# Softmax factors transposed by VectorE in 32 by 32 blocks instead of by TensorE

## The chip, the cores and the metric

The kernel runs on one core of a Trainium2 chip. A core has five engines, each with its own stream of instructions, which run side by side and wait for each other by semaphores: TensorE (PE, matrix multiply into PSUM), VectorE (DVE), ScalarE (ACT), GpSimd (POOL) and SyncE (SP, which here issues all transfers). The metric is the device time of one execution in microseconds; lower is better. Before the change it is 962.03 us, the median of 3 runs (960.35 to 965.0).

## The reference

Three stages follow one another. The first is a causal attention over 4 batches with 8 heads, 576 positions and 64 channels, with a bias from a running sum:

```python
scores = scale * np.matmul(q, k.transpose(0, 1, 3, 2))
cum = np.cumsum(np.maximum(s, 0.0), axis=-1)
bias = -(cum[:, :, :, None] - cum[:, :, None, :])
scores = np.where(causal, -1000000000.0, scores + np.minimum(bias, 0.0))
scores = scores - np.max(scores, axis=-1, keepdims=True)
attn = np.exp(scores)
attn = attn / (np.sum(attn, axis=-1, keepdims=True) + 1e-09)
return np.matmul(attn, v).astype(np.float32)
```

The heads are then joined to x of 2304 tokens by 512 channels. The second stage computes h = x @ w_in (512 by 2048), g = h * cos(h) and g @ w_out. The third normalises by the root of the mean square, multiplies by w_gate and w_val (512 by 1536 each), takes silu(gate) * value and multiplies by w_out2.

## The kernel before

The attention works on 16 pairs of heads. For a pair TensorE computes the scores of query blocks of 128 rows (`score`, line 541, and `score_p`, line 565), VectorE adds the bias and takes the row maximum (lines 548 and 568), ScalarE takes the exponential and the row sums (line 576), TensorE transposes the exponentials (line 591), VectorE or ScalarE copies them out of PSUM into `Pa` and `Pb` (lines 341 and 344), and TensorE multiplies them with v (line 625), which gives the unnormalised result of both heads, channels along partitions, in `xu`. The matrix multiplies of the two feed-forward stages are split into seven products instead of eight, by Strassen's and Winograd's scheme, and in float32r with a high and a low part (lines 842, 1007, 1074 and 1220).

The division by the row sums comes last. The sums of a pair lie in `rs`, 128 rows by 9 columns, one column for each block of queries. `factors` adds the small constant and takes the reciprocal on VectorE (lines 503 and 505), transposes the 128x9 tile with TensorE (line 506) into nine rows of 128, copies these out of PSUM into `rt` (line 341) and writes them to a row `rn_d` in device memory. From there three transfers spread them over the partitions into `rb`, of which there is one buffer. `store` multiplies `xu` by `rb` on VectorE and sends the product to `x_d`, from which the first feed-forward loads.

No order is written out by hand. All operations are given to a planner, `Plan`, with a nominal duration, the tiles that they read and write, and a priority: a due time `plan.now` plus an offset such as `O_FACTOR`. It simulates the engines and issues, on each, the ready operation of the lowest priority value. Where a copy may run on ScalarE or VectorE, the planner chooses the one that it expects to be done first. So the numbers at the head of the file (`P_ATT` is the spacing of the pairs, `W2_FROM` the due time of the first load of w_out, `LEAD_O` the lead of another) decide the order of the program, while the waits between engines follow from the tiles. SyncE issues transfers strictly in the planner's order.

Of the kernel before, what the change touches and what calls it, by code (L numbers as in the profile page):

```python
# [10 lines left out]
F32 = mybir.dt.float32  # L11
# [3 lines left out]
ALU = mybir.AluOpType  # L15
# [10 lines left out]
PAIRS1, PAIRS2 = F1 // 2, F2 // 2  # L26
WARM = 10
DEPTH = 2
LEAD_I, LEAD_O, LEAD_E = 11929.0, 9594.0, 0.0
SWITCH_PE = 95.0  # L30
KEEP_MODE = 1671.0
DMA_EACH, DMA_RATE, DMA_LATE = 5.0, 20.64, 2101.0
DS_AT = 0.0
TWO_PI = 6.283185
HALF_PI = 1.5707962
BIG = 1.0e9
SIZES = {}
P_ATT, P_SET, P_MM, P_OUT = 10969.0, 7380.0, 2110.0, 2145.0
T_FF1 = 179007.0
LAST_PAIRS = 1  # L40
W1_FROM, W1_EACH, W2_FROM, W2_EACH = 38376.0, 23365.0, 236432.0, 17377.0
XA0, XA1, XA2, XB0, XB1, XB2 = 107519.0, 169410.0, 213287.0, -34206.0, -16987.0, 7443.0
XR2, XR3, XR5 = -8690.0, 5219.0, 3642.0
YT_FROM, YT_EACH, YS_FROM, YS_EACH = -3234.0, 7175.0, 9960.0, 11025.0
LEAD_W, LEAD_C, LEAD_S, LEAD_R, XG0, XG1, XG2 = -6032.0, 11731.0, -984.0, 14881.0, 3264.0, 419.0, 1965.0
O_LOAD, O_BIAS, O_V, O_MASK, O_SCORE, O_TTR, O_RAGGED = -9957.0, -3314.0, -825.0, 3187.0, -6310.0, -102.0, -4260.0
O_EXP, O_TR, O_P, O_PV, O_X, O_FACTOR, O_STORE = 704.0, -96.0, 175.0, 4486.0, 4432.0, 969.0, -6809.0
O_VALUE, O_GEMM1, O_GEMM2, O_SIN, O_X1 = 534.0, 0.0, 0.0, 37.0, 0.0

# [80 lines left out]
class Plan:  # L132
    SEM = {"PE": 200.0, "ACT": 140.0, "DVE": 140.0, "POOL": 140.0, "SP": 0.0}
    SAME = {"PE": 0.0, "ACT": 110.0, "DVE": 127.0, "POOL": 104.0, "SP": 0.0}
    WEIGH = {"PE": 1.0, "ACT": 1.0, "DVE": 2.23, "POOL": 0.86, "SP": 1.0}
    SWITCH, HOLD = 1283.0, 30592.0

    def __init__(self):
        self.ops, self.rings, self.arenas, self.now = [], [], [], 0.0
# [147 lines left out]
def attention_moe_moe(ctx, tc, qk, vp, s, w_in, w_out, w_gate, w_val, w_out2, rms_g, out):  # L287
    nc = tc.nc
    pe, act, dve, pool, sp = nc.tensor, nc.scalar, nc.vector, nc.gpsimd, nc.sync
    plan = Plan()  # L290
# [13 lines left out]
    def ring(name, n, shape, dtype, where="main"):  # L304
        n = SIZES.get(name, n)
        def make(slot):
            if where not in pools:
                first, kw = ends[where]
                stacks[first].close()
                pools[where] = spool(ctx, where, **kw)  # L310
            return pools[where].tile(shape, dtype, name=f"{name}{slot}", tag=f"{name}{slot}")

        r = Ring(plan, make, n)
        if where in ("main", "att", "early"):
            for i in range(n):
                r.tile(i)
        return r
# [17 lines left out]
    def on(e, ns, fn):  # L335
        return [(e, ns, fn)]

    def copy(o, i, n, r, w, scale=1.0, psum=False, engines=("ACT", "DVE"), **kw):
        alts = []
        if "ACT" in engines:  # L340
            alts.append(("ACT", (act_p if psum else act_s)(n), lambda: act.activation(o(), i(), AF.Copy, scale=scale)))  # L341
        if "DVE" in engines:
            if scale == 1.0:
                alts.append(("DVE", (dve1 if psum else dve2)(n), lambda: dve.tensor_copy(o(), i())))
            else:
                alts.append(("DVE", dve2(n), lambda: dve.tensor_scalar(out=o(), in0=i(), scalar1=scale, scalar2=None, op0=ALU.mult)))
        if "POOL" in engines:
            alts.append(("POOL", pool1(n), lambda: pool.tensor_scalar(out=o(), in0=i(), scalar1=scale, scalar2=0.0, op0=ALU.mult, op1=ALU.add)))
        return plan.op(alts, r, w, port=not psum, **kw)
# [59 lines left out]
    xu_r = ring("xu", 3, [128, S], F32, "att")  # L409
    p_r = {"a": ring("Pa", 2, [128, 384], F32, "att"), "b": ring("Pb", 2, [128, 4, 320], F32, "att")}  # L410
    mn_r = ring("mn", 2, [128, 10], F32, "att")
    rs_r = ring("rs", 2, [128, 9], F32, "att")
    rt_r = ring("rt", 1, [128, 128], F32, "att")
    rb_r = ring("rb", 1, [128, S], F32, "att")
    c_d, ce_d = dbuf("c_d", [B * H, S]), dbuf("ce_d", [B * H, 512])
    rn_d = [dbuf(f"rn_d{i}", [1, 1152]) for i in range(B * NP)]
# [29 lines left out]
    class Run:  # L446
# [51 lines left out]
            return psb("first", (0, 1, 2, 3, 4, 5, 6, 7)) if self.bp < B * NP - LAST_PAIRS else psb("att", (4, 5, 6, 7))  # L498

        def factors(self):  # L500
            rs, tr, rt = self.rs, self.bank(), rt_r.new()
            dst = rn_d[self.bp]
            plan.op(on("DVE", 130, lambda: dve.tensor_scalar(
                out=rs(), in0=rs(), scalar1=1e-9, scalar2=float(2.0 * np.pi), op0=ALU.add, op1=ALU.mult)), [], [rs], prio=O_FACTOR)
            plan.op(on("DVE", 204, lambda: dve.reciprocal(out=rs(), in_=rs())), [], [rs], prio=O_FACTOR)
            plan.op(on("PE", 109, lambda: pe.transpose(tr()[:9, :128], rs(), ident)), [rs], [tr], rows=0.1, prio=O_FACTOR)
            copy(lambda: rt()[:9, :], lambda: tr()[:9, :128], 128, [tr], [rt], psum=True, prio=O_FACTOR)
            load(lambda: dst().rearrange("a (b c) -> (a b) c", c=128), lambda: rt()[:9, :], 4608, [rt], [dst], run=512, prio=O_FACTOR)
            rb = self.rb = rb_r.new()
            for e, lo, hi, o in ((0, 0, S, 0), (1, 0, 512, 640), (1, 512, S, 64)):  # L510
                load(lambda e=e, lo=lo, hi=hi: rb()[64 * e:64 * e + 64, lo:hi], lambda lo=lo, hi=hi, o=o: dst()[0, o + lo:o + hi].partition_broadcast(64),
                     256 * (hi - lo), [dst], [(rb, (e, lo))], run=min(4 * (hi - lo), 4096), prio=O_FACTOR)

    class Part:
# [65 lines left out]
        def tr(self, e, i):  # L580
            tr = self.bank("T")
            if e not in self.P:
                self.P[e] = p_r[self.c].new()
            srcs = {0: [((e, 0), 0, 128), ((e, 1), 0, 128), ((e, 1), 128, 128)], 1: [((e, 2), 128 * c, 128) for c in range(3)] + [("p", 512, 128)] * (e == 0),
                    2: [((e, 3), 128 * c, 128) for c in range(4)], 3: [("p", 128 * c, 128) for c in range(4)]}[i]
            P = self.P[e]
            Es = [self.E[k] for k, _, _ in srcs]

            def go():
                for j, ((k, c, m), E) in enumerate(zip(srcs, Es)):  # L590
                    pe.transpose(tr()[:m, 128 * j:128 * j + 128], E[0]()[:, E[2] + c:E[2] + c + m], ident)  # L591

            plan.op(on("PE", 109 * len(srcs), go), [(E[0], E[1]) for E in Es], [tr], rows=0.5, prio=O_TR)
            cols = lambda n: tr()[:, :n].rearrange("p (c i) -> p c i", i=128)
            def out(o, src, n, P=P):
                copy(o, src, n, [tr], [P], psum=True, prio=O_P)

            if i == 0:
                out(P, lambda: tr()[:, 0:384], 384)
            elif i == 1:  # L600
                out(lambda: P()[:, 0:3, 0:128], lambda: cols(384), 384)
                for a in range(2) if e == 0 else ():
                    out(lambda a=a: self.P[a]()[:, 3, 0:64], lambda a=a: tr()[:, 384 + 64 * a:448 + 64 * a], 64, self.P[a])
            elif i == 2:
                out(lambda: P()[:, :, 128:256], lambda: cols(512), 512)
            else:
                for a in range(2):
                    out(lambda a=a: self.P[a]()[:, :, 256:320], lambda a=a: cols(512)[:, :, 64 * a:64 * a + 64], 256, self.P[a])
# [36 lines left out]
                   [*(lambda e=e, i=i: self.tr(e, i) for e, i in ((0, 1), (1, 1), (0, 3)))], False, True)  # L645

    runs = [Run(bp, "ab") for bp in range(B * NP)]

    def merged(a, b):
        n = [(i + 0.5) / len(a) for i in range(len(a))] + [(i + 0.75) / len(b) for i in range(len(b))]  # L650
# [653 lines left out]
```

## Time and profile before

| what | before |
|---|---|
| median of 3 runs | 962.03 us |
| the profiled execution, own time | 960.69 us |
| its span, from first to last instruction | 958.9 us |
| PE busy | 947.1 us (99%) |
| DVE busy | 802.7 us (84%) |
| ACT busy | 597.5 us (62%) |
| POOL busy | 136.5 us (14%) |
| mean granted PE clock | 1.000 |

A busy share is that of the whole span. The stages have different limits, so shares of one stretch say more. The ends of matmuls are modelled, so a PE that is busy all the time may still issue less than it could.

### The profile page before, as it was taken

What the parts mean: (1) busy time and instruction counts of PE and PEld (TensorE: products, weight loads), DVE (VectorE), ACT (ScalarE), POOL (GpSimd) and SP (SyncE); (2) the same over time, 40 slices, a digit from 0 to 9 for tenths busy, and PEclk for the clock granted to TensorE, in tenths of its full rate; (3) what the DMA queues carried; (4) which work ended last, traced back from release to release, by engine and by line L of the source; (5) the groups of instructions that cost most, each with busy time, mean ns of one, the idle gap of its engine ahead of it and who ended that gap; (6) DMA issues with size and microseconds to landing.
All of it is one profiled execution on the core that took longest, in us unless ns stands there. A gap on an engine that the chain in (4) does not pass through costs nothing.

```text
span 958.9 us, 18412 instructions
## 1 busy us (share of the span) xinstructions
PE 947.1 (99%) x5990; PEld 878.2 (92%) x5990; DVE 802.7 (84%) x1796; ACT 597.5 (62%) x1319; POOL 136.5 (14%) x267
## 2 busy tenths in 40 slices
PE   9999999999999999999999989999999999999998
PEld 5666666899999999999999979999999999999998
DVE  5999899999999899886779999988878767886661
ACT  5999999887777683352557465644536346675540
POOL 4544443102132000000000101111101000000000
PEclk9999999999999999999999999999999999999999
DMA  7899998659788799986773825677566758997761
GB/s 228 286 294 304 339 296 288 233 178 302 256 305 286 235 368 310 324 309 198 218 230 109 291 84 185 208 225 236 160 199 177 209 170 260 319 324 228 214 181 44
DMA packets 155760, 230.34 MB, mean 240 GB/s; under 512 B 15648, under 2 KB 112560, under 8 KB 155664
## 3 DMA queue, kind: packets, MB, share of 16 engines
q1 hardware_dynamic: 155664, 229.16, 74.2%
q8 instruction: 47, 0.77, 0.3%
q14 instruction: 49, 0.40, 0.1%
HBM read 150.51 MB, written 78.59 MB: 239 GB/s over the span
## 4 chain that ended last, share of the span: by engine, by line
PE 88%; DVE 5%; ACT 2%; DMA 2%; issue 2%; SPq 1%; POOL 0%; DVEq 0%; POOLq 0%; ACTq 0%
PE banks L842 41%; PE banks L1007 14%; PE banks L1220 13%; PE banks L1074 6%; PE banks L591 4%; PE banks L625 4%; PE banks L541 4%; DVE wk L352 2%; PE banks L565 1%; SPq L356 1%; DMA rb<-rn_d 1%; DMA wk<-g_d 1%; DVE wg L352 1%; ACT e L576 1%; DMA wi<-w_o 0%
## 5 line engine op out<-in xcount | busy, mean ns | idle before, releaser
L842 PE MATMUL banks<-wi,wg 128*128 128x384 f32 x882 | 175.4, 338 | 3.8 <-DVE wk L352 1.4
L842 PEld LDWEIGHTS banks<-wi,wg 128*128 128x128 f32 x882 | 154.2, 188 | 8.4 <-ACT banks L874 3.2
L352 DVE TENSOR_TENSOR wk<-wk 128x256 f32<-128x256 f32 (+1 forms) x258 | 118.9, 487 | 4.9 <-ACT wk L953 3.6
L432 POOL TENSOR_SCALAR wk<-wk 128x512 f32<-128x512 f32 x68 | 57.9, 852 | 427.6 <-ACT wk L429 228.5
L352 DVE TENSOR_TENSOR wk<-wk,banks 128x256 f32<-128x256 f32 (+1 forms) x111 | 70.8, 647 | 46.4 <-PE banks L1220 41.8
L842 PE MATMUL banks<-wr,wg 128*128 128x384 f32 x588 | 107.4, 338 | 0.0
L842 PEld LDWEIGHTS banks<-wr,wg 128*128 128x128 f32 x588 | 103.2, 188 | 1.0 <-DVE banks L352 0.2
L874 ACT COPY banks<-banks 128x384 f32<-128x384 f32 x124 | 58.2, 469 | 62.1 <-PE banks L842 53.8
L341 ACT ACTIVATE wg<-wg 128x384 fp32r<-128x384 f32 (+2 forms) x140 | 70.3, 525 | 42.6 <-DMA wg<-g_d 26.9
L352 DVE TENSOR_TENSOR banks<-banks,wk 128x384 f32<-128x384 f32 x122 | 68.0, 558 | 31.4 <-ACT banks L874 20.8
L352 DVE TENSOR_TENSOR wg<-wg 128x384 fp32r<-128x384 f32 (+2 forms) x140 | 77.6, 577 | 19.7 <-ACT wg L341 19.5
L352 DVE TENSOR_TENSOR wk<-banks,wk 128x768 f32<-128x768 f32 (+1 forms) x86 | 80.3, 940 | 4.8 <-PE banks L842 3.4
L842 PE MATMUL banks<-wi,wz 128*128 128x384 f32 x378 | 75.2, 337 | 2.1 <-ACT wk L1139 1.5
L576 ACT ACTIVATE e<-e,mn 128x512 f32<-128x512 f32 (+3 forms) x128 | 70.7, 560 | 5.2 <-DVE mn L548 4.9
L1007 PE MATMUL banks<-wg,wr 128*128 128x384 f32 x408 | 73.4, 338 | 0.0
L1007 PEld LDWEIGHTS banks<-wg,wr 128*128 128x128 f32 x408 | 71.9, 188 | 0.0
L842 PEld LDWEIGHTS banks<-wi,wz 128*128 128x128 f32 x378 | 66.1, 188 | 3.8 <-ACT wk L1139 1.9
L842 PE MATMUL banks<-we,wg 128*128 128x384 f32 x294 | 67.8, 339 | 0.0
L1220 PE MATMUL banks<-wi,wr 128*128 128x256 f32 x501 | 62.0, 282 | 0.6 <-DVE wi L352 0.6
L1220 PEld LDWEIGHTS banks<-wi,wr 128*128 128x128 f32 x501 | 60.4, 188 | 1.2 <-DVE wi L352 1.0
L548 DVE CUSTOM_DVE_ANT_0 e<-banks,ce 128x512 f32<-128x512 f32 (+2 forms) x96 | 49.8, 551 | 12.3 <-PE banks L541 7.1
L914 ACT ACTIVATE wk<-banks,quarter 128x768 int32<-128x768 f32 x48 | 43.1, 900 | 22.8 <-PE banks L842 21.9
(158 smaller groups left out, 1857.7 us busy)
## 6 DMA issues: line engine op xcount, KB each, us to landing
g_d<-wk SPq DMA_DIRECT2D x48, 384.0 KB, 4.3
wg<-g_d SPq DMA_DIRECT2D x75, 192.0 KB, 3.7
wk<-in_w_out_dram SPq DMA_DIRECT2D x28, 512.0 KB, 4.8
g_S<-wk SPq DMA_DIRECT2D x72, 192.0 KB, 3.8
g<-wk SPq DMA_DIRECT2D x54, 192.0 KB, 3.7
qk<-in_qk_dram SPq DMA_DIRECT2D x16, 608.0 KB, 5.2
wk<-in_w_in_dram SPq DMA_DIRECT2D x16, 512.0 KB, 7.3
wr<-g_S SPq DMA_DIRECT2D x41, 192.0 KB, 2.7
```

The lines of the kernel that those rows point to most:

```text
L341: alts.append(("ACT", (act_p if psum else act_s)(n), lambda: act.activation(o(), i(), AF.Copy, scale=scale)))
L352: return plan.op(on("DVE", dve1(n), lambda: dve.tensor_tensor(out=o(), in0=a(), in1=b(), op=op)), r, w, port=not psum, **kw)
L432: plan.op(on("POOL", 610, lambda: pool.tensor_scalar(out=top().bitcast(F32), in0=top().bitcast(F32), scalar1=0.0, scalar2=1.0, op0=ALU.mul ...
L541: pe.matmul(Sp[e]()[:, o:o + w], run.q()[hd, q0:q0 + 128], run.k()[hd, :w], start=True, stop=True)
L548: plan.op(on("DVE", dve1(w) + 17, lambda t=t, o=o, w=w, i=i, e=e: dve.tensor_tensor_reduce(out=Es[e]()[:, o:o + w], in0=Sp[e]()[:, o:o + w ...
L576: plan.op(on("ACT", act_s(w) + 187, lambda E=E, o=o, w=w, i=i, c=c: act.activation(E()[:, o:o + w], E()[:, o:o + w], AF.Exp, scale=-1.0, b ...
L842: pe.matmul(bank_()[:, :HALF2], G[i]()[:, u, o + 128 * k:o + 128 * k + 128], xs[k]()[:, c, :], start=(first and n == 0), stop=(n == 5), sk ...
L874: plan.op(on("ACT", act_p(HALF2), lambda: act.copy(o(), i())), r, w)
L914: plan.op(on("ACT", act_p(m) + 93, lambda: act.activation(dst().bitcast(I32), src(), AF.Identity, bias=quarter)), [x, y], w)
L1007: pe.matmul(to[k]()[:, :HALF2], w()[:, c, 128 * k:128 * k + 128], g()[:, a, :], start=(first and a == 0 and c == 0), stop=(last and a == 1 ...
L1074: pe.matmul(to()[:, :HALF2], w()[:, c, o:o + 128], g()[:, a_, :], start=(first and a_ == 0 and c == 0), stop=(last and a_ == 1), skip_grou ...
L1220: pe.matmul(bk_()[:, col:col + 256], gs[p // 3]()[:, u, 128 * (p % 3):128 * (p % 3) + 128], w3[p][i]()[:, c, o:o + 256], start=(n == 0), s ...
```

## The change

The tile `rs` becomes 128x32, of which the last 23 columns are set to zero once for each of its two buffers. VectorE transposes it in blocks of 32 by 32, so that block g of the partitions holds the nine factors' rows of queries 32g to 32g + 31 of every block. The matmul, the PSUM bank and the copy out of it go. Four transfers, one for each group of 32 partitions, write nine runs of 128 bytes each, where one transfer wrote nine runs of 512 bytes. `rt` gets a second buffer. The broadcast and the multiply stay as they are. Beside this, some forty numbers that set due times and priorities have other values.

```diff
-LEAD_I, LEAD_O, LEAD_E = 11929.0, 9594.0, 0.0
+LEAD_I, LEAD_O, LEAD_E = 11929.0, 12003.0, 0.0
...
-W1_FROM, W1_EACH, W2_FROM, W2_EACH = 38376.0, 23365.0, 236432.0, 17377.0
+W1_FROM, W1_EACH, W2_FROM, W2_EACH = 38376.0, 23365.0, 230751.0, 17737.0
...
-    rs_r = ring("rs", 2, [128, 9], F32, "att")
-    rt_r = ring("rt", 1, [128, 128], F32, "att")
+    rs_r = ring("rs", 2, [128, 32], F32, "att")
+    rt_r = ring("rt", 2, [128, 32], F32, "att")
...
-            rs, tr, rt = self.rs, self.bank(), rt_r.new()
+            rs, rt = self.rs, rt_r.new()
             dst = rn_d[self.bp]
...
-            plan.op(on("DVE", 204, lambda: dve.reciprocal(out=rs(), in_=rs())), [], [rs], prio=O_FACTOR)
-            plan.op(on("PE", 109, lambda: pe.transpose(tr()[:9, :128], rs(), ident)), [rs], [tr], rows=0.1, prio=O_FACTOR)
-            copy(lambda: rt()[:9, :], lambda: tr()[:9, :128], 128, [tr], [rt], psum=True, prio=O_FACTOR)
-            load(lambda: dst().rearrange("a (b c) -> (a b) c", c=128), lambda: rt()[:9, :], 4608, [rt], [dst], run=512, prio=O_FACTOR)
+            plan.op(on("DVE", 204, lambda: dve.reciprocal(out=rs()[:, :9], in_=rs()[:, :9])), [], [rs], prio=O_FACTOR)
+            plan.op(on("DVE", 100, lambda: dve.transpose(out=rt(), in_=rs())), [rs], [rt], prio=O_FACTOR)
+            for g in range(4):
+                load(lambda g=g: dst().rearrange("a (j g i) -> (a j) g i", g=4, i=32)[:, g, :], lambda g=g: rt()[32 * g:32 * g + 9, :], 1152, [rt], [(dst, g)], run=128, prio=O_FACTOR)
...
+    for _ in range(2):
+        clear = rs_r.new()
+        plan.op(on("POOL", 100, lambda clear=clear: pool.memset(clear()[:, 9:], 0.0)), [], [clear])
```

The order of the instructions moves with it, above all in the attention. On TensorE, in the middle of the attention before, the transpose of the factors (line 506, from `rs`) stands between the scores of one pair and the transposes of the exponentials of another (line 591):

```order
L541 MATMUL banks<-qk_97 128x128 x2
L541 MATMUL banks<-qk_97 128x256 x2
L506 MATMUL banks<-ident,rs_122 9x128
L591 MATMUL banks<-ident,e_109 128x128 x4
L591 MATMUL banks<-ident,e_110 128x128 x4
L591 MATMUL banks<-ident,e_107 128x128 x3
```

On TensorE after, at the same place in the pair of heads:

```order
L541 MATMUL banks<-qk_97 128x128 x2
L541 MATMUL banks<-qk_97 128x256 x2
L565 MATMUL banks<-qk_97 128x288
L591 MATMUL banks<-ident,e_109 128x128 x4
L591 MATMUL banks<-ident,e_110 128x128 x4
```

The transpose of the factors is gone, and here the scores of the last, ragged block (line 565) come ahead of the transposes.

On VectorE in the fourth pair before, the reciprocal (line 505) stands one instruction behind the addition (line 503), ahead of the bias and maximum of the scores (lines 548 and 568, shown as ISA; `e`, `mn` and `ce` are the exponentials' tile, the maxima and the bias):

```order
L435 SCALAR_TENSOR_TENSOR wk<-wk 128x512
L503 TENSOR_SCALAR rs_123<-rs_123 128x9
L352 TENSOR_TENSOR wk<-wk 128x256
L505 RECIPROCAL rs_123<-rs_123 128x9
L548 ISA e_109,mn_120<-banks,ce_100 128x512
```

On VectorE after, there, with the new transpose (line 506):

```order
L503 TENSOR_SCALAR rs_123<-rs_123 128x9
L352 TENSOR_TENSOR wk<-wk 128x256
L548 ISA e_109,mn_120<-banks,ce_100 128x512
...
L505 RECIPROCAL rs_123<-rs_123 128x9
L344 COPY xu_113<-banks 128x256
L506 STREAM_TRANSPOSE rt_125<-rs_123 128x32
L352 TENSOR_TENSOR wk<-wk 128x256 x3
```

The reciprocal has moved behind the six score instructions of the next unit, and the transpose follows it after one copy out of PSUM.

On SyncE at the tenth pair before, the store of the ninth product (`x_d<-xu`) is followed at once by the three broadcasts of the tenth pair's factors (`rb<-rn_d`):

```order
L356 DMA rn_d_137<-rt_124 9x128
L356 DMA ce_100<-ce_d 128x1024
L356 DMA wi<-x_d 128x384
L356 DMA cp_102<-c_d 64x576 x2
L356 DMA qk_97<-in_qk_dram 128x1216
L356 DMA cp_103<-c_d 64x576 x2
L356 DMA w_4_169<-wk 128x256
L356 DMA x_d<-xu_115 128x576
L356 DMA rb_125<-rn_d_137 64x576
```

On SyncE after, at the same pair:

```order
L356 DMA x_d<-xu_115 128x576
L356 DMA rn_d_138<-rt_125 9x32
L356 DMA ce_100<-ce_d 128x1024
L356 DMA cp_102<-c_d 64x576 x2
L356 DMA wk<-in_w_in_dram 128x1024
L356 DMA rn_d_139<-rt_124 9x32 x2
L356 DMA rb_126<-rn_d_138 64x576
```

Here seven transfers, three of them writes of factors, have come between the store and the broadcast.

## Rows read from the trace of the kernel before

**Rows 1.** The page, busy time of each engine, share, instructions.
```profile
PE 947.1 (99%) x5990; PEld 878.2 (92%) x5990; DVE 802.7 (84%) x1796; ACT 597.5 (62%) x1319; POOL 136.5 (14%) x267
```

**Rows 2.** Busy time by stretch: length, then each engine's us, clock, DMA share, GB/s.
```profile
20.00:160.00 140.00, 138.86 (x1044) 90.34 (x1043) 130.59 (x454) 133.12 (x430) 65.76 (x162) 1.00 0.93 300
...
180.00:300.00 120.00, 118.81 (x666) 115.69 (x665) 118.31 (x177) 90.72 (x146) 20.39 (x27) 1.00 0.74 255
300.00:400.00 100.00, 98.71 (x559) 97.30 (x559) 90.92 (x168) 62.22 (x109) 4.33 (x6) 1.00 0.89 308
...
500.00:600.00 100.00, 96.52 (x546) 94.88 (x545) 94.98 (x222) 58.39 (x124) 8.53 (x7) 1.00 0.53 172
```

**Rows 3.** The chain of waits, 100 to 111 us: start, length, what.
```profile
100.91 2.21 PE banks L625 x20
...
103.97 0.21 PE banks L506
104.18 1.64 PE banks L591 x15
...
109.74 0.97 PE banks L565 x4
110.71 0.11 PE banks L506
```

**Rows 4.** The tile rt: count, ns min/median/max, first and last start.
```profile
L341 ACT ACTIVATE rt<-banks x16: 247/250/267, 25.3 to 171.8; 9x128 f32<-9x128 f32 x16
L356 SPq DMA_DIRECT2D rn_d<-rt x16: 286/296/516, 25.6 to 174.4; - x16
```

**Rows 5.** The chain of waits, 178 to 275 us.
```profile
181.18 0.94 DVE wk L352
...
189.38 47.98 PE banks L842 x270
...
237.87 2.33 DVE wg L352 x3
```

**Rows 6.** Groups by line and form, 0 to 190 us: busy us, mean ns, idle before.
```profile
L548 DVE DVE_READ_ACCUMULATOR2_ANT mn<- 128x1 f32 x128 | 10.4, 81 | 0.0
...
L344 DVE COPY Pb<-banks 128x384 f32<-128x384 f32 x13 | 7.1, 549 | 0.3 <-PE banks L591 0.3
...
L344 DVE COPY Pb<-banks 128x64 f32<-128x64 f32 x19 | 3.5, 212 | 0.0
...
L505 DVE RECIPROCAL rs<-rs 128x9 f32<-128x9 f32 x16 | 3.3, 207 | 0.0
...
L506 PEld LDWEIGHTS banks<-ident,rs 128*9 128x9 f32 x16 | 1.4, 88 | 4.7 <-issue 1.1 <-ACT ep L576 1.0 <-DVE mn L548 0.8
```

**Rows 7.** Line 981, VectorE's transpose of 384 columns.
```profile
L981 DVE STREAM_TRANSPOSE wk<-st x6: 566/569/578, 401.1 to 564.9; 128x384 f32<-128x384 f32 x6
```

**Rows 8.** Instructions in order of time, 126 to 135 us, SyncE and VectorE.
```profile
126.54 1.79 SPq L356 DMA_DIRECT2D rb<-rn_d  x3
...
129.72 0.29 SPq L356 DMA_DIRECT2D rn_d<-rt  x1
130.17 0.45 SPq L356 DMA_DIRECT2D ce<-ce_d  x1
...
132.61 0.76 DVE L352 TENSOR_TENSOR xu<-xu,rb 128x576 f32<-128x576 f32 x1
...
134.46 0.40 SPq L356 DMA_DIRECT2D x_d<-xu  x1
134.91 0.59 SPq L356 DMA_DIRECT2D rb<-rn_d  x1
```

**Rows 9.** Waits, 0 to 190 us: us in total, times, longest.
```profile
SPq L356 <- DVE xu L352: 11.8, 10, 4.3
...
SPq L356 <- DMA rn_d<-rt: 5.7, 4, 2.9
...
DVE xu L352 <- DMA rb<-rn_d: 2.9, 3, 1.2
```

More of the change, by code (lines that the diff above doesn't have):

```diff
@@ L28 @@
 DEPTH = 2
-LEAD_I, LEAD_O, LEAD_E = 11929.0, 9594.0, 0.0
+LEAD_I, LEAD_O, LEAD_E = 11929.0, 12003.0, 0.0
 SWITCH_PE = 95.0
 KEEP_MODE = 1671.0
-DMA_EACH, DMA_RATE, DMA_LATE = 5.0, 20.64, 2101.0
+DMA_EACH, DMA_RATE, DMA_LATE = 5.0, 20.14, 2101.0
 DS_AT = 0.0
@@ L37 @@
 SIZES = {}
-P_ATT, P_SET, P_MM, P_OUT = 10969.0, 7380.0, 2110.0, 2145.0
+P_ATT, P_SET, P_MM, P_OUT = 11032.0, 7380.0, 2110.0, 2145.0
 T_FF1 = 179007.0
 LAST_PAIRS = 1
-W1_FROM, W1_EACH, W2_FROM, W2_EACH = 38376.0, 23365.0, 236432.0, 17377.0
[L42 to L48, printed above, removed]
+W1_FROM, W1_EACH, W2_FROM, W2_EACH = 38376.0, 23365.0, 230751.0, 17737.0
+XA0, XA1, XA2, XB0, XB1, XB2 = 107519.0, 169410.0, 217796.0, -31143.0, -19100.0, 3241.0
+XR2, XR3, XR5 = -12387.0, 7821.0, 3642.0
+YT_FROM, YT_EACH, YS_FROM, YS_EACH = -149.0, 10058.0, 8639.0, 10597.0
+LEAD_W, LEAD_C, LEAD_S, LEAD_R, XG0, XG1, XG2 = -6032.0, 11090.0, -984.0, 14159.0, 3264.0, 419.0, 1965.0
+O_LOAD, O_BIAS, O_V, O_MASK, O_SCORE, O_TTR, O_RAGGED = -9957.0, -1945.0, 856.0, 4953.0, -6310.0, 1156.0, -4260.0
+O_EXP, O_TR, O_P, O_PV, O_X, O_FACTOR, O_STORE = 704.0, -96.0, 175.0, 4486.0, 4432.0, 969.0, -9906.0
+O_VALUE, O_GEMM1, O_GEMM2, O_SIN, O_X1 = 997.0, 0.0, 0.0, -1233.0, 0.0
 class Op:
@@ L135 @@
     WEIGH = {"PE": 1.0, "ACT": 1.0, "DVE": 2.23, "POOL": 0.86, "SP": 1.0}
-    SWITCH, HOLD = 1283.0, 30592.0
+    SWITCH, HOLD = 1283.0, 23338.0
     def __init__(self):
@@ L500, in factors @@
         def factors(self):
-            rs, tr, rt = self.rs, self.bank(), rt_r.new()
+            rs, rt = self.rs, rt_r.new()
             dst = rn_d[self.bp]
             plan.op(on("DVE", 130, lambda: dve.tensor_scalar(
-                out=rs(), in0=rs(), scalar1=1e-9, scalar2=float(2.0 * np.pi), op0=ALU.add, op1=ALU.mult)), [], [rs], prio=O_FACTOR)
-            plan.op(on("DVE", 204, lambda: dve.reciprocal(out=rs(), in_=rs())), [], [rs], prio=O_FACTOR)
-            plan.op(on("PE", 109, lambda: pe.transpose(tr()[:9, :128], rs(), ident)), [rs], [tr], rows=0.1, prio=O_FACTOR)
-            copy(lambda: rt()[:9, :], lambda: tr()[:9, :128], 128, [tr], [rt], psum=True, prio=O_FACTOR)
-            load(lambda: dst().rearrange("a (b c) -> (a b) c", c=128), lambda: rt()[:9, :], 4608, [rt], [dst], run=512, prio=O_FACTOR)
+                out=rs()[:, :9], in0=rs()[:, :9], scalar1=1e-9, scalar2=float(2.0 * np.pi), op0=ALU.add, op1=ALU.mult)), [], [rs], prio=O_FACTOR)
+            plan.op(on("DVE", 204, lambda: dve.reciprocal(out=rs()[:, :9], in_=rs()[:, :9])), [], [rs], prio=O_FACTOR)
+            plan.op(on("DVE", 100, lambda: dve.transpose(out=rt(), in_=rs())), [rs], [rt], prio=O_FACTOR)
+            for g in range(4):
+                load(lambda g=g: dst().rearrange("a (j g i) -> (a j) g i", g=4, i=32)[:, g, :], lambda g=g: rt()[32 * g:32 * g + 9, :], 1152, [rt], [(dst, g)], run=128, prio=O_FACTOR)
             rb = self.rb = rb_r.new()
```

## The prediction

> **What bounds the kernel now.** I began with the busy shares of the engines. TensorE is busy for 947.1 of 958.9 us [rows 1], so whatever the change does to the other engines counts only where TensorE waits for them or is relieved itself. The second view was the busy time by stretch, since the change lies in the attention, the first 180 us. The reader is to see there that from 20 to 160 us no engine has much to spare: TensorE 138.86 of 140, ScalarE 133.12, VectorE 130.59, the DMA engines 93%. After it VectorE is the tight one up to 300 us (118.31 of 120), and TensorE's lost time is 1.2, 1.3 and 3.5 us in the three stretches shown [rows 2]. The third view was the chain of waits. Within one pair of heads, from 100.91 to 110.82 us, it runs on TensorE without a break [rows 3]: 9.91 us. The writes of the softmax factors, one per pair, start from 25.6 to 174.4 us, 15 steps of 9.92 us [rows 4]. So a pair lasts as long as TensorE's work for it, and the attention is bound by TensorE with three others close behind. From 181 to 270 us the chain goes through VectorE three times before TensorE takes over again; one of these places and the run of matmuls before it are shown [rows 5].
>
> **The change, part by part.**
>
> TensorE loses 16 transposes of the factors, one per pair. In the chain they stand as pieces of 0.21 and 0.11 us [rows 3]. The longer one holds a wait that the next transpose would have had as well, so I take 0.11: 16 x 0.11 = 1.8 us off the bounding engine. The lower bound is nothing. The upper bound takes the weight loads and all the idle time before them, 1.4 + 4.7 = 6.1 us [rows 6].
>
> ScalarE loses 16 copies of 0.250 us [rows 4], 4.0 us. TensorE bounds the pair, so I count nothing for it; the bounds are 0 and -4.0 us.
>
> VectorE gains 16 transposes of 128x32, which the trace does not show in this size. A copy out of PSUM takes 212 ns at 64 columns and 549 ns at 384 [rows 6], 1.05 ns a column, so 32 columns would be 178 ns. The kernel's own transpose of 384 columns takes 569 ns [rows 7]; 352 columns less make it 0.20 us. The smallest VectorE instruction of the attention takes 81 ns [rows 6]. I take 0.18: 16 x 0.18 = 2.9 us, within 1.3 (81 ns each) and 3.4 (212 ns each). The cover is VectorE's own idle time in the attention, 140 - 130.59 = 9.4 us [rows 2]. If that idle time can't be used (it lies between dependent instructions), the 2.9 us are passed on to the stretch up to 300 us, where only 1.7 us are free. The Trainium skill (VectorE: DVE Perf Modes, the section on the fixed extra latency of ops that read SBUF) has a table row of 58 + columns cycles at 0.96 GHz, which would make this transpose an estimated 94 ns and the 16 of them 1.5 us; the same section says that the row under-predicts single operations, and the rows here side with that.
>
> The replanned copies: counted in the two orders, five 64-wide copies and one 384-wide copy move from VectorE to ScalarE and three 256-wide ones the other way. At 0.21, 0.55 and (by the same slope) 0.41 us that is -1.1 - 0.5 + 1.2 = -0.4 us on VectorE. I count nothing.
>
> SyncE gets 48 more issues of 0.296 us [rows 4], 0.89 us a pair. What can be late through it is a loop through one buffer: the broadcast of the factors may be issued only when the multiply of the pair before has read that buffer. In the trace it goes broadcast issued at 126.54, multiply at 132.61 to 133.37, its store issued at 134.46, next broadcast at 134.91 [rows 8]: 8.37 us against a cadence of 9.92. By the two orders, the transfers that stand between the store and the next broadcast rise from 14 to 36 over 15 gaps, 1.5 a pair, at 0.29 to 0.45 us each [rows 8] some 0.6 us. The loop then takes 9.0 us, still 0.9 below the cadence. So I count nothing; if the three extra writes fall into it in full it is 9.9 us, and the cover is gone. What is queued behind a late broadcast is the store of the pair and the loads of the next one on SyncE, and on VectorE, which runs in order, all that stands behind the multiply. The factors themselves have time: TensorE's transpose at 110.71 us [rows 3] is the tenth, and the tenth broadcast is the one issued at 126.54 us [rows 8], 15.8 us later.
>
> The shape of the write speaks against the change: nine rows of 512 bytes become 36 of 128. The trace shows SyncE waiting for this write 4 times, 5.7 us in all [rows 9]. The Trainium skill (DMA: Bandwidth & Descriptors, Specifications) puts the smallest transfer at full rate at 512 bytes and says that below it the engine reads, modifies and writes; no run here shows yet what this costs. By that rule the wait would lengthen, which is the slow rival below.
>
> The two memsets on GpSimd stand at the start, before the identity matrix. By the nearest small instruction, a reciprocal of 207 ns [rows 6], they are at most 0.4 us, while TensorE warms up. I count nothing. The second buffer for the transposed factors takes a wait away that I can't see in the trace.
>
> The retuned numbers move work in the whole program. After the attention TensorE's order stays nearly the same (weights and products in the same sequence), so this can win back at most the idle time there, 1.2 + 1.3 + 3.5 = 6.0 us [rows 2], and I allow a loss of 4.7, the first and the last of these doubled. I take 0: nothing in the trace tells the sign.
>
> The sum: -1.8 us. The profiled execution took 960.69 us (span 958.9), so 958.9 us is the forecast. The median of the three runs, 962.03, lies 1.3 us above that execution.
>
> **The rivals.**
>
> Given back. The attention becomes shorter, but VectorE, with 2.9 - 0.4 = 2.5 us more work, delivers the first feed-forward's operands no earlier, or later. For it: the chain's pieces on VectorE at 237.87 us and its 118.31 of 120 us. Against: 9.4 us idle before. TensorE then gains 1.8 and waits up to 1.8 + 2.5 more: 960.7 to 963.2 us, say 962.
>
> Faster. TensorE's waits before the removed transposes go as well (6.1 us), since ScalarE and a bank are freed too: 960.69 - 6.1 = 954.6 us. With half of the 6.0 us behind the attention it is 951.6. For it: the idle time before the weight loads is listed as waits for ScalarE and VectorE. Against: other waits for the same engines follow at once, and the pieces of the chain leave no gap.
>
> Slower. The broadcast loop becomes the bound of the attention. It decides from the point where broadcast to broadcast takes over 9.92 us: 8.37 + 0.6 + 0.89 = 9.86 with the three writes inside, and two gaps have 7 and 5 transfers in between. Half a microsecond beyond it is 16 x 0.5 = 8 us: 960.69 + 8 = 968.7 us. For it: VectorE already waits 2.9 us for the broadcast, three times [rows 9], and SyncE waits 11.8 us for the multiply [rows 9], so both ends of the loop touch. Against: the free 0.9 us.
>
> **How the numbers follow.** Forecast 0.36, given back 0.20, faster 0.27, slower 0.17. A measurement of this kernel can tell about 0.5% from no change, here 4.8 us: below 957.2 is faster, above 966.8 slower. Forecast and given back are both within it. So faster 0.27, same 0.56, slower 0.17. The forecast's own range, from the bounds of TensorE's share, VectorE's cost and a small part of the reordering, is 956 to 962. The range for 8 in 10 reaches into the faster case to 952 and into the slower one to 967.5.
>
> **What would show it.** The factor writes' cadence should fall by about 0.1 us from 9.92, and TensorE's last attention matmul should come 1 to 2 us earlier. VectorE's new transpose should be near 0.18 us, and its busy time from 20 to 160 us should rise while its idle time shrinks. TensorE's idle time from 180 to 300 us should stay near 1.2 us; if it grows by 2 us, the gain was given back. VectorE's wait for the broadcast should stay near 2.9 us; if it grows several times over, the loop was the bound. A change of over 3 us that arises only after 300 us would make the reasoning wrong, since nothing but the retuned numbers acts there.

## The result and the profile after

The changed kernel takes 970.85 us (median of 6 runs, 969.49 to 974.91) where the kernel before takes 960.66 us (6 runs, 958.05 to 965.0): a ratio of 1.0104, 95% interval 1.0077 to 1.0131. It is slower by 10 us, where 958.9 was forecast and the range ended at 967.5. One execution in this document, pe_four's at 984.07 us, was a slow run and is left out of the figures.

The page after answers to [rows 1]: busy time of each engine, its share, its instructions.

```profile
PE 950.2 (98%) x5974; PEld 879.8 (91%) x5974; DVE 802.7 (83%) x1810; ACT 594.7 (61%) x1304; POOL 134.7 (14%) x270
```

The span went from 958.9 to 971.3 us (this execution took 973.12 us, 2.3 above the median), while TensorE's busy time rose by 3.1: the rest is waiting. Where it waits is seen in the busy time by stretch after, which answers to [rows 2] (length, each engine's us, clock, DMA share, GB/s).

```profile
20.00:160.00 140.00, 134.02 (x974) 86.11 (x971) 120.57 (x429) 124.32 (x393) 59.32 (x150) 0.99 0.88 272
180.00:300.00 120.00, 114.99 (x646) 110.21 (x645) 112.69 (x176) 87.97 (x144) 22.34 (x30) 0.99 0.75 258
300.00:400.00 100.00, 98.72 (x553) 95.89 (x552) 93.95 (x159) 65.79 (x110) 7.12 (x11) 1.00 0.87 302
500.00:600.00 100.00, 96.42 (x544) 94.49 (x543) 91.70 (x216) 60.17 (x129) 5.07 (x5) 1.00 0.58 183
```

From 20 to 160 us every engine is less busy than before, and so are the DMA engines (93% to 88%). When all are idler at once, none of them has become the bound: something holds up the loop over the pairs as a whole. From 300 us on, TensorE's busy time in the two stretches shown is as before.

The tile of the factors after answers to [rows 4] (count, ns min/median/max, first and last start).

```profile
L506 DVE STREAM_TRANSPOSE rt<-rs x16: 198/205/213, 20.9 to 178.0; 128x32 f32<-128x32 f32 x16
L356 SPq DMA_DIRECT2D rn_d<-rt x64: 264/307/2183, 21.4 to 185.3; - x64
```

The multiply by the factors, one a pair, gives the cadence. Of the kernel before:

```profile
L352 DVE TENSOR_TENSOR xu<-xu,rb x16: 742/759/1233, 36.6 to 186.4; 128x576 f32<-128x576 f32 x16
```

and after, with VectorE's wait behind it (us in total, times), which was 2.9 in 3 [rows 9]:

```profile
L352 DVE TENSOR_TENSOR xu<-xu,rb x16: 744/756/1194, 31.3 to 196.4; 128x576 f32<-128x576 f32 x16
...
  DMA rb<-rn_d: 7.9, 5
```

Fifteen steps take 165.1 us instead of 149.8: 11.01 a pair instead of 9.99. The last multiply is 10.0 us late, of 12.4 us that the span grew. The transposes of the last stage, first and last start, show the rest; they answer to [rows 7]:

```profile
L984 DVE STREAM_TRANSPOSE wk<-st x6: 566/577/578, 413.5 to 577.4; 128x384 f32<-128x384 f32 x6
```

The first was at 401.1, so all 12.4 us are there by then; the last, then at 564.9, is 12.5 late.

What holds the loop is read from the chain of waits after, 70 to 92 us (start, length, what). In the kernel before, this stretch of the chain runs on TensorE but for one stop at VectorE, much as in [rows 3]; here it runs through transfers.

```profile
70.97 7.81 DMA rb<-rn_d
78.78 0.02 issue
78.79 0.26 SPq L356
...
79.16 6.61 DMA ce<-ce_d
85.76 0.02 issue
85.78 5.89 DMA rb<-rn_d
```

and from SyncE's instructions in order of time there (start, length, what, count):

```profile
70.97 1.82 SPq L356 DMA_DIRECT2D rb<-rn_d  x3
73.48 0.29 SPq L356 DMA_DIRECT2D rn_d<-rt  x1
74.23 0.34 SPq L356 DMA_DIRECT2D qk<-in_qk_dram  x1
76.25 0.94 SPq L356 DMA_DIRECT2D rn_d<-rt  x2
78.26 0.36 SPq L356 DMA_DIRECT2D vr<-in_vp_dram  x1
78.79 0.26 SPq L356 DMA_DIRECT2D rn_d<-rt  x1
79.16 0.34 SPq L356 DMA_DIRECT2D ce<-ce_d  x1
79.54 1.09 SPq L356 DMA_DIRECT2D cp<-c_d  x2
80.74 0.52 SPq L356 DMA_DIRECT2D x_d<-xu  x1
81.31 0.42 SPq L356 DMA_DIRECT2D wi<-x_d  x1
81.78 0.47 SPq L356 DMA_DIRECT2D wk<-in_w_in_dram  x1
82.34 3.88 SPq L356 DMA_DIRECT2D rb<-rn_d  x3
```

The third broadcast, at 85.78 us, reads nothing that `ce<-ce_d` writes, yet it starts when that load, issued at 79.16, has landed. Count the transfers from it on: ce, cp, cp, x_d, wi, wk, rb, rb. It is the eighth before. The last factor write, at 78.79, likewise starts when a broadcast issued from 70.97 on has landed. The order of the instructions says why: in this program each transfer of SyncE signals one of eight semaphores (DMAHW0 to 7) in turn, and waits until the transfer eight places before it, which used the same one, has landed. The same stretch of SyncE's order, with what each waits for:

```
L356 DMA rn_d_134<-rt_125 9x32 [waits DMAHW6_49]
L356 DMA ce_100<-ce_d 128x1024 [waits DMAHW7_49,DVE_49]
L356 DMA cp_102<-c_d 64x576 [waits DMAHW0_49]
L356 DMA cp_102<-c_d 64x576 [waits DMAHW1_49]
L356 DMA x_d<-xu_114 128x576 [waits DMAHW2_49,DVE_49,Activation_49]
L356 DMA wi<-x_d 128x384 [waits DMAHW3_49]
L356 DMA wk<-in_w_in_dram 128x1024 [waits DMAHW4_49]
L356 DMA rb_126<-rn_d_134 64x576 [waits DMAHW6_49,DMAHW5_49]
L356 DMA rb_126<-rn_d_134 64x512
L356 DMA rb_126<-rn_d_134 64x64 [waits DMAHW7_49]
```

So in this program SyncE has a window of eight transfers in flight. A transfer costs not only its 0.3 us of issue but a place among eight until it lands, 5.9 to 7.8 us in the chain above, and the change raises the transfers up to the last product's store from 207 to 254, 12.9 to 15.9 a pair. One row shows the window at work. No transfer reads `qk`, so where SyncE waits for the landing of a `qk` load, only the window can be the reason. SyncE's waits from 0 to 190 us (us in total, times, longest) before, and after:

```profile
SPq L356 <- DMA qk<-in_qk_dram: 3.3, 3, 2.0
```
```profile
SPq L356 <- DMA qk<-in_qk_dram: 7.1, 8, 1.4
```

### The profile page after: what moved, and what is told of

Its sections match the earlier page's. It is cut to its first block, busy times and chain, and to the rows that moved or that the text cites. A ratio compares the mean times of both kernels' runs of the same rounds, so it can differ in the third digit from the quotient of the medians.

```text
span 971.3 us, 18399 instructions
## 1 busy us (share of the span) xinstructions
PE 950.2 (98%) x5974; PEld 879.8 (91%) x5974; DVE 802.7 (83%) x1810; ACT 594.7 (61%) x1304; POOL 134.7 (14%) x270
## 4 chain that ended last, share of the span: by engine, by line
PE 80%; DMA 6%; ACT 4%; DVE 4%; issue 3%; SPq 1%; POOL 1%; POOLq 0%; DVEq 0%; ACTq 0%
PE banks L845 39%; PE banks L1010 13%; PE banks L1223 12%; PE banks L1077 6%; PE banks L625 3%; PE banks L541 3%; PE banks L591 3%; DMA rb<-rn_d 2%; DMA ce<-ce_d 1%; ACT wk L919 1%; SPq L356 1%; ACT wk L917 1%; PE banks L565 1%; DMA wi<-w_o 1%; DVE wk L352 1%
## 5 line engine op out<-in xcount | busy, mean ns | idle before, releaser
L432 POOL TENSOR_SCALAR wk<-wk 128x512 f32<-128x512 f32 x68 | 54.8, 806 | 426.6 <-ACT wk L429 300.6
L845 PE MATMUL banks<-wr,wg 128*128 128x384 f32 x588 | 110.0, 342 | 1.9 <-ACT banks L877 1.8
L352 DVE TENSOR_TENSOR wg<-wg 128x384 fp32r<-128x384 f32 (+2 forms) x140 | 75.4, 562 | 20.3 <-ACT wg L341 20.1
```

What stands on the lines that cost most here:

```text
L352: return plan.op(on("DVE", dve1(n), lambda: dve.tensor_tensor(out=o(), in0=a(), in1=b(), op=op)), r, w, port=not psum, **kw)
L432: plan.op(on("POOL", 610, lambda: pool.tensor_scalar(out=top().bitcast(F32), in0=top().bitcast(F32), scalar1=0.0, scalar2=1.0, op0=ALU.mul ...
L845: pe.matmul(bank_()[:, :HALF2], G[i]()[:, u, o + 128 * k:o + 128 * k + 128], xs[k]()[:, c, :], start=(first and n == 0), stop=(n == 5), sk ...
```

## The experiments

The expectations were written before each run. In them theory 1 is that the three more transfers a pair cost the time, through the places that they take on SyncE. The rivals are theory 2, the new numbers and the new order; theory 3, VectorE's added transposes; and theory 4, the small writes' own cost. All ratios are to the kernel before, with 95% intervals. "Held" means that every engine keeps the kernel before's order: the planner is given the old operations, and only what they emit is exchanged.

**The change cut in two.** numbers_alone has the old operations and all new numbers (25 values differ, not some forty); structure_alone has the new operations and the old numbers.

```diff
-O_LOAD, O_BIAS, O_V, O_MASK = -9957.0, -3314.0, -825.0, 3187.0
+O_LOAD, O_BIAS, O_V, O_MASK = -9957.0, -1945.0, 856.0, 4953.0
```

> Before's operations, planned with the new numbers; one factor write a pair. Theory 1 (the window: a transfer on SyncE's queue waits for the landing of the eighth before it, and three more transfers a pair fill that window): 958 to 964 us, about before's 960.7. Theory 2 (the retuned numbers give a bad order): 968 to 973 us, about the changed kernel's 970.9. Theory 3 (VectorE's added transposes push back its other work): 958 to 964 us.

> The new operations, planned with the old numbers. Theory 1 (window): 966 to 974 us, since the four writes a pair are there. Theory 2 (numbers): 958 to 963 us. Theory 3 (VectorE): 964 to 971 us.

Measured: 966.45 us, 1.0057 (1.0038 to 1.0077), and 979.93 us, 1.0207 (1.0174 to 1.024). Both halves cost, and structure_alone more than the whole: the new numbers win back about 1% (9 to 10 us) of what the new operations lose under the old ones, but cost 0.6% (5.5 us) without them. Neither expectation was met cleanly, and the next runs therefore hold the order.

**Held order, four writes.** held_four takes VectorE's transpose and the four writes; pe_four keeps TensorE's transpose and splits only the write.

```diff
 # held_four
-pe.transpose(tr()[:9, :128], rs(), ident)
-(copy of tr to rt)
-sp.dma_start(out=dst().rearrange("a (b c) -> (a b) c", c=128), in_=rt()[:9, :])
+dve.transpose(out=to, in_=rs())
+for g in range(4):
+    sp.dma_start(out=dst().rearrange("a (j g i) -> (a j) g i", g=4, i=32)[:, g, :], in_=to[32 * g:32 * g + 9, :])
 # pe_four: the write alone
+for g in range(4):
+    sp.dma_start(out=dst().rearrange("a (j g i) -> (a j) g i", g=4, i=32)[:, g, :], in_=rt()[:9, 32 * g:32 * g + 32])
```

> Before's order held instruction by instruction on all engines; TensorE's transpose and the copy out of PSUM are left out, VectorE's transpose follows the reciprocal, and four writes stand where one stood. Theory 1 (window): 966 to 976 us, and SyncE waits longer for transfers eight places back. Theory 2 (numbers and order): 959 to 961 us. Theory 3 (VectorE): 962 to 966 us, 16 x 0.205 us = 3.3 us of VectorE at most, less TensorE's 1.8.

> Before's order held; TensorE transposes and the copy stay, only the one write of nine rows of 512 bytes becomes four of nine rows of 128 bytes, one behind the other. Theory 1 (window): 966 to 976 us, as held_four or a little above. Theory 2 and theory 3: 960 to 962 us, no more than the 0.9 us of issue a pair can hide.

Measured: 971.42 us, 1.0124 (1.0082 to 1.0165), and 972.02 us, 1.0105 (1.0055 to 1.0155). With the order held, splitting one write into four costs about as much as the whole change, whoever transposes. SyncE's waits from 0 to 190 us, of held_four and then of pe_four:

```profile
SPq L356 <- DMA qk<-in_qk_dram: 11.5, 9, 2.6
```
```profile
SPq L356 <- DMA qk<-in_qk_dram: 11.8, 9, 2.4
...
SPq L356 <- DMA rn_d<-rt: 5.0, 7, 2.5
```

The wait that only the window explains is three and a half times that of before (held_one below, which loses nothing that can be told, has 5.5 us of it in 4), while the wait for the factor write itself is not longer than the 5.7 us of [rows 9]. The row tells that the window binds, not what it costs: pe_two and held_less below, which lose nothing that can be told either, have 9.2 us of it in 7 and 9.4 in 8, in profiled executions that were the longest of their ten (967.56 and 966.24 us).

**Held order, one write.** held_one has VectorE's transpose and a single write of 36 runs of 128 bytes.

```diff
-for g in range(4): (four writes)
+sp.dma_start(out=dst().rearrange("a (j g i) -> (a j) g i", g=4, i=32), in_=to[:9, :].unsqueeze(1).to_broadcast([9, 4, 32]))
```

> Before's order held, TensorE's transpose and the copy left out, VectorE's transpose in, and one write a pair of 36 runs of 128 bytes in place of four writes of nine such runs. It writes the first 32 queries' factors four times over, so three quarters of the rows are divided by a wrong factor: that part of the computation is changed, the work and the bytes are not. Theory 1 (the number of transfers in the window of eight): 956 to 962 us, no slower than before's 960.2, perhaps 1 to 3 us faster. Theory 3 (VectorE's transposes): 962 to 965 us. Theory 4 (writes of 128 bytes take long on the DMA engines): 966 to 972 us, as held_four.

Measured: 961.1 us, 1.0008 (0.9985 to 1.0031). SyncE takes longer to issue this write, 0.83 us where the old one took 0.296 [rows 4] (one of its two buffers, ns min/median/max):

```profile
L512 SPq DMA_DIRECT2D rn_d<-rt_b x8: 822/828/835, 29.6 to 173.5; - x8
```

That is 8.5 us more over the 16 pairs, against 14.9 for four writes of 0.307. dve_one does the same with complete factors: one write of all 128 partitions, 128 runs of 128 bytes, to longer rows.

```diff
+sp.dma_start(out=dst().rearrange("a (j g i) -> (a g) j i", g=4, i=32), in_=to)
```

> Before's order held, VectorE's transposes, and one write a pair of all 128 partitions (128 runs of 128 bytes, 16 KB) to a larger row, so the result is the whole one. Theory 1 (number of transfers): 958 to 963 us, as the kernel that wrote 36 runs in one transfer (961.1). If bytes or runs of the write count: 964 us and more.

Measured: 963.15 us, 1.0037 (1.0014 to 1.0059). So VectorE's transposes, TensorE's and ScalarE's relief, runs of 128 bytes and 8.5 us more of SyncE's issue time together move the time by nothing that can be told (held_one), and 128 such runs a write, issued in 0.57 us, cost 0.1 to 0.6%. The Trainium skill (DMA: Bandwidth & Descriptors, Specifications) has transfers below 512 bytes read, modify and write; what that costs here lies within these bounds.

**The dose.** pe_two and pe_eight split the write of pe_four into 2 and 8, that is 1 and 7 more transfers a pair at the same bytes.

```diff
-for g in range(4):
+for g in range(k):   # k = 2, and k = 8
```

> Before with TensorE's transposes, order held; the one factor write a pair becomes two of nine rows of 256 bytes. Theory 1 (each transfer takes one of eight places until it lands): a third of the loss of the four writes or less, 960.5 to 965 us. If only SyncE's issue time counts (0.3 us more a pair), 960 to 961.5 us. If writes below 512 bytes are the cost, 965 us and more.

> Before with TensorE's transposes, order held, the one factor write a pair becomes eight of nine rows of 64 bytes. Theory 1 (places in the window): seven more transfers a pair; two writes cost 1.3 us, four 10 us, so once the window is full each further transfer costs about 4 us over the 16 pairs: 983 to 1005 us. If the loss of the four writes came from one bad place in the order: 970 to 978 us.

Measured: 962.25 us, 1.0014 (0.9988 to 1.004), and 1000.32 us, 1.042 (1.04 to 1.044). With one more transfer a pair nothing can be told, with three 10 to 12 us are lost, with seven 40 us. The multiplies of pe_eight show the loop stretched (15 steps, 191.1 us, 12.74 a pair), and its writes have runs of 64 bytes, whose own price was not measured alone:

```profile
L352 DVE TENSOR_TENSOR xu<-xu,rb x16: 746/758/847, 37.1 to 228.2; 128x576 f32<-128x576 f32 x16
```

held_less goes the other way: held_four, but with two other transfers a pair left out (the narrow broadcast of the factors, and one head's broadcast of the running sum).

```diff
-load(rb()[64:128, 512:S] ...)
-load(cp()[64:128, :] ...)
```

> Before's order held, VectorE's transposes and the four writes kept, but two other transfers a pair are left out: the 64-wide part of the broadcast (16 KB) and the second head's ragged bias (144 KB), in whose place zeros stand, so the last 64 queries of each second head are wrong. One transfer a pair more than before, as with two writes. Theory 1: 958 to 964 us, as with two writes (962.3). If the four writes themselves are the cost: 968 to 972 us.

Measured: 961.8 us, 1.0014 (0.9992 to 1.0035). Four small writes, but one transfer more in the sum, and the loss is gone. It takes 160 KB a pair away as well; pe_four, at unchanged bytes, is the cleaner proof, and the two agree.

**Other queues.** held_pool and held_act issue the four writes from GpSimd and from ScalarE; pe_pool is the kernel before with its one write issued from GpSimd.

```diff
-    sp.dma_start(...)
+    pool.dma_start(...)   # held_pool, pe_pool; act.dma_start in held_act
```

> Before's order held, VectorE's transposes, and the four writes issued from GpSimd, which has a window of its own; SyncE issues one transfer a pair less than before and three less than the four-write kernel. Theory 1 (window): 956 to 963 us, unless GpSimd is slowed by issuing them. Theory 4 (128-byte writes): 966 to 972 us. If GpSimd's issue of 64 transfers delays its masks, VectorE's wait for GpSimd's ce and m tiles grows from before's 4.0 us to over 8 us and the time lies at 964 to 972 us.

> Before's order held, VectorE's transposes, and the four writes issued from ScalarE, which shares the eight semaphores of the window with SyncE. Theory 1 in its form 'the landing of the eighth transfer before': 966 to 976 us, no better than the same kernel with the writes on SyncE (971.4), with the waits now also on ScalarE. Theory 1 in its form 'SyncE's issue time': 957 to 963 us, since SyncE's 64 issues are gone.

> Before with TensorE's transposes, order held; only its one factor write a pair goes from SyncE to GpSimd, which takes one transfer a pair out of SyncE's window. Theory 1 (window): 957 to 960.5 us, the same or up to 3 us faster than before. If the window does not matter: 959.5 to 962 us.

Measured: 969.59 us, 1.0098 (1.0067 to 1.013); 982.46 us, 1.0241 (1.0196 to 1.0286); 960.03 us, 0.9999 (0.9976 to 1.0022). The first two don't win the loss back; in each, another wait has grown. A write costs GpSimd 0.52 us where it costs SyncE 0.31, and VectorE then waits for GpSimd's bias tile (0 to 190 us, held_pool):

```profile
DVE e L560 <- POOL ce L484: 11.8, 11, 1.7
```

where the same wait was 4.0 us before. SyncE waits for the factor writes there for 19.5 us (13.5 and 6.0 for the two buffers of `rt`), against 5.7 before [rows 9]. ScalarE signals the same eight semaphores in turn, so its writes take places in the same window, and now ScalarE itself stops for the landing of an earlier one (0 to 200 us, held_act):

```profile
ACT e L588 <- DMA rn_d<-rt_b: 11.2, 3, 5.7
```

So these two neither prove nor break theory 1. pe_pool frees a place a pair and gains nothing: with the old count, as far as this run tells, a freed place is worth nothing, though SyncE waits longer for the write itself in it (14.0 us in 8).

**Fewer transfers by merging.** held_merged and after_merged put the three broadcasts of the factors into two and the two of the running sum into one, with a source of two rows.

```diff
+sp.dma_start(out=rb()[:, 0:512], in_=bass.AP(s.tensor, s.offset, [[640, 2], [0, 64], [1, 512]]))
```

> Before's order held, VectorE's transposes and four writes as in the held four-write kernel (971.4 us), but the three broadcasts of the factors are two over both heads and the two broadcasts of the ragged bias are one, with the same bytes: three more and two fewer transfers a pair. Theory 1 (number of transfers): most of the 11 us comes back, 960 to 965 us. Theory 4 (the small writes themselves, or their landing ahead of the broadcast): 968 to 972 us.

> The changed kernel's order held, all four writes kept, the broadcasts merged (two fewer transfers a pair, same bytes). Theory 1: 960 to 966 us, most of the loss of 10 us comes back. If the four writes themselves are the cost: 969 to 972 us.

Measured: 1106.03 us, 1.1506 (1.147 to 1.1542), and 1105.81 us, 1.151 (1.1479 to 1.154). A failed idea: the merged transfers are waited for far longer. GpSimd's wait for the merged one, 0 to 190 us of held_merged (before: 8.0 us, longest 2.7):

```profile
POOL cp L481 <- DMA cp<-c_d: 92.7, 10, 13.9
```

Both also give partly wrong values, and why is not shown. These two say nothing on theory 1.

**The new order.** after_one keeps the changed kernel's order and lets only the last of its four writes issue, as held_one's single one (a quarter of the factors is right). after_early is the changed kernel with the broadcasts moved directly behind the store before them.

```diff
 # after_one
-for g in range(4): load(...)
+for g in range(4): plan.op(on("SP", 475.0, write if g == 3 else lambda: None), ...)
 # after_early
+order.remove(o)
+order.insert(order.index(after) + 1, o)   # o: the three broadcasts; after: the store or the last write
```

> The changed kernel's order held, but only one factor write a pair, of 36 runs of 128 bytes, at the place of the last of the four. It writes the first 32 queries' factors four times over, so three quarters of the rows are divided by a wrong factor: that part of the computation is changed. Theory 1 (number of transfers): 958 to 965 us, near before and what the new numbers alone cost (966.5 with one write). Theory 2 (the new order is bad in itself): 968 to 971 us.

> The changed kernel's order, complete, but on SyncE the three broadcasts of a pair are moved directly behind the store of the pair before (36 transfers stood in between over 15 pairs, now 1). If the lengthened broadcast loop is what the new order costs: 960 to 966 us. If it is the number of transfers and the rest of the order: 968 to 974 us, since what is behind the broadcasts comes later by as much.

Measured: 968.47 us, 1.0083 (1.0051 to 1.0115), a miss for theory 1, which wanted the loss gone; and 980.35 us, 1.0214 (1.0196 to 1.0232). In the changed kernel's order, then, taking the three transfers away wins 2 us, which the intervals do not even separate from nothing: 8 of the 10 us stay. The order itself is a second cause. (The one write takes SyncE 0.82 us here, so three places and 0.41 us of issue a pair are taken away.)

Where each cause sits is seen when the step from one pair's first broadcast to the next pair's is divided, by SyncE's and VectorE's instructions in order of time (means of 15 steps, us):

| run | broadcast to the multiply's end | to the store's issue | to the next broadcast | step |
|---|---|---|---|---|
| before | 8.24 | 0.27 | 1.57 | 10.08 |
| held_one | 8.05 | 0.45 | 1.71 | 10.21 |
| held_four | 7.62 | 1.99 | 1.36 | 10.97 |
| pe_four | 7.64 | 1.76 | 1.44 | 10.83 |
| after | 8.13 | 0.49 | 2.35 | 10.97 |
| after_one | 8.31 | 0.19 | 2.30 | 10.80 |
| after_early | 8.86 | 0.87 | 1.68 | 11.41 |

In the old order, four writes make SyncE late for the store, and the way from the store to the broadcast gets no longer. In the new order that way is longer by 0.7 to 0.8 us, with four writes and with one: over the 15 steps 36 and 33 transfers lie on it, where 14 did. So this is where the changed kernel's step grew. That it is what costs the 8 us isn't shown: with the broadcasts moved forward the way is short again and the kernel slower still, since SyncE then stops for the factor writes (0 to 190 us, after_early; 1.1 us in 3 in the changed kernel):

```profile
SPq L356 <- DMA rn_d<-rt: 16.7, 10, 4.5
```

**Planned anew with one write.** one_new and one_old give the planner dve_one's single write in place of the four, with the new and with the old numbers.

```diff
-for g in range(4): load(...)
+load(lambda: dst().rearrange("a (j g i) -> (a g) j i", g=4, i=32), lambda: rt(), 16384, [rt], [dst], run=128, prio=O_FACTOR)
```

> The changed kernel with one write a pair of all 128 partitions instead of four, complete, planned anew with the new numbers. If the changed kernel's order lost its 8 us because it was laid out for three more transfers: 958 to 963 us. If the new numbers are bad for one write whatever the transposes: 964 to 969 us, as before's operations with the new numbers (966.5).

> The same kernel, one write a pair, planned anew with the old numbers. If transfers are the cause of what the new structure cost with the old numbers (979.9 with four writes): 958 to 964 us. If planning VectorE's transposes with the old numbers gives a bad order in itself: 970 us and more.

Measured: 977.42 us, 1.0173 (1.0139 to 1.0208), and 978.31 us, 1.0193 (1.015 to 1.0237). Both missed. In both, the attention is sound: the last multiply starts at 185.5 and 185.6 us, earlier than before. The loss lies behind it. Busy time by stretch of one_old:

```profile
0.00:200.00 200.00, 194.48 (x1349) 133.05 (x1350) 175.07 (x572) 172.53 (x511) 81.17 (x202) 1.00 0.89 285
200.00:300.00 100.00, 91.42 (x500) 89.22 (x499) 93.20 (x140) 69.49 (x113) 20.61 (x28) 0.97 0.69 243
```

and of dve_one, the same operations in the held order:

```profile
0.00:200.00 200.00, 194.69 (x1358) 133.35 (x1359) 180.67 (x583) 172.92 (x509) 75.64 (x201) 1.00 0.88 284
200.00:300.00 100.00, 99.39 (x560) 97.21 (x559) 98.08 (x146) 77.06 (x125) 19.01 (x26) 1.00 0.74 257
```

To 200 us they are equal; in the next 100 us TensorE is busy 8 us less, at a lower clock (0.97). With other operations in the attention the planner puts the first feed-forward's work in another order too, and the 8 us there are most of what four writes cost in the attention.

## Why the prediction was wrong

The step that failed is the one on SyncE: "SyncE gets 48 more issues of 0.296 us [rows 4], 0.89 us a pair. [...] So I count nothing". The price of an issue was right (0.307 us now), and so, nearly, was the longer way from store to broadcast (0.6 us a pair forecast, 0.78 in the table above). Wrong was the cover of 0.9 us. The 8.37 us of [rows 8] from one broadcast to the next are a single step, taken for the length of the loop. Before, the 15 steps go from 6.50 to 12.51 us; their mean is the cadence, whatever bounds it, and shows no room. Two of the longer ones, 11.33 and 12.51 us, on SyncE before (start, length, what):

```profile
58.47 1.93 SPq L356 DMA_DIRECT2D rb<-rn_d  x3
...
69.80 1.74 SPq L356 DMA_DIRECT2D rb<-rn_d  x3
...
82.31 1.73 SPq L356 DMA_DIRECT2D rb<-rn_d  x3
```

And a transfer was priced by its issue and followed through this one loop, not by its place among the eight in flight. At equal order this step is worth 10 to 12 us (held_four, pe_four), and nothing that can be told once the count is back near the old one (held_one, held_less).

A second step failed too: "The retuned numbers move work in the whole program. [...] I take 0", with a loss of 4.7 us as its bound. The numbers alone cost 5.5 us (0.57%). The changed kernel's order, which the new numbers and the new operations make together, costs 8 us with one write (after_one), and orders planned for one write 15 to 19 (one_new, one_old). In the changed kernel the two causes overlap and do not add: of about 10 us in all, the three transfers directly hold some 2 and the order the rest, as far as after_one tells.

The other steps. TensorE's 1.8 us and ScalarE's 4.0 were worth nothing that can be told: held_one has both, and 1.0008. The forecast let TensorE's share count in full because the chain ran on TensorE alone; what took it up is not shown, since held_one also has VectorE's transposes and the longer issue. VectorE's transpose takes 205 ns, not 180: the value by slope from the 384-column transpose (0.20) was the better of the two. The 94 ns estimated from the Trainium skill's row (VectorE: DVE Perf Modes, the section on the fixed extra latency) is less than half of what was measured. VectorE's cover held (held_one). The small runs cost nothing that can be told; the prediction had them lengthen SyncE's wait for the write, which is 1.1 us in 3 now. TensorE's idle time from 180 to 300 us, named as the sign of a gain given back, went from 1.2 to 5.0 us; part of that stretch is attention now, since the last multiply starts at 196.4 us. That the time after 300 us would stay as it was, was right.

The slow rival had the sign, the size (968.7) and the engine, SyncE's queue, and was given 0.17. Its mechanism, the longer way from store to broadcast, is in the changed kernel's trace (1.57 to 2.35 us a pair), but not in held_four and pe_four, which lose as much. Its cost is not shown, since after_early, which takes it away, meets another wait. The signs named for it did appear (VectorE's wait for the broadcast, 2.9 us in 3 multiplies before, 7.9 in 5 of 16 after; a cadence above 9.92), and they would appear for any late transfer; they don't tell the loop from the window. The window's own sign is a landing that nothing needs, and that row was there to be read before (`qk`, 3.3 us in 3).

The granted clock is a part of it, not the cause. In the changed kernel it falls from 80 to 100 us, where TensorE was waiting in the chain shown:

```profile
80.00:100.00 20.00, 16.53 (x112) 9.56 (x108) 14.16 (x51) 13.14 (x40) 7.50 (x20) 0.91 0.86 250
```

In one group of 28 matmuls there the chain counts 4.02 us at 94.44, against 2.86 at 81.52 us in the kernel before. But pe_four loses 1.05% with its profiled execution at a mean clock of 1.000.

Open stays through which instructions the new orders lose their 5 to 19 us. Only the places are known: the way from store to broadcast in the changed kernel, 160 to 200 us in numbers_alone (TensorE busy for 36.29 us at a clock of 0.91, 39.46 at 1.00 before), 200 to 300 us in one_new and one_old. Open also is how much of the 10 to 12 us at equal order is the window and how much SyncE's issue time, 16 x 3 x 0.307 = 14.7 us: the chain and the `qk` waits show the window at work, and the issues from ScalarE, which should have told the two apart, loaded ScalarE. held_one gives an estimate: its 8.5 us more of issue were covered. If that cover is the same for all, issue time accounts for about 6 of the 14.9 us that four writes add, and 25 of the 33.4 that eight add (0.298 us each), where 10 to 12 and 40 were lost; the rest would be the window's. No version tried beats the kernel before; pe_pool, held_one, pe_two, held_less and dve_one come within 0.4% of it.

## What to carry to other kernels

Before splitting a transfer, count the transfers a queue has in flight and what they take to land: where a loop keeps a fixed window nearly full, each further transfer costs a place until landing, however few its bytes, and a wait of the queue for a load that no later transfer reads is the sign that the window binds, though not of what it costs. One step read off a trace is not the length of a loop: look at all of them, and read the room from the waits, since the mean step is the cadence in any case. An order that a planner makes is part of the tuning: to judge an edit, hold the order and exchange only what is emitted, then judge the new order by itself. When all engines are less busy at once after a change, look at the queues first.

## What the runs showed of the hardware that was not expected

A write of 36 runs of 128 bytes left the time as it was with 9 runs of 512 (1.0008, 0.9985 to 1.0031), though it kept SyncE 0.83 us in place of 0.296 to issue; one of 128 such runs, from all 128 partitions, kept it 0.57 us. A broadcast to 128 partitions from two source rows kept GpSimd waiting up to 13.9 us where two to 64 partitions each kept it 2.7 at most. A write of nine such runs issued from GpSimd takes it 521 ns (median of 32), from SyncE 307 (of 64), from ScalarE 326 and 274 (of 32 from each of the two buffers).
